# Seven block products for a pair of chunks in the first expert, half-wide products for the last group, and Silu in one instruction

## The chip, the cores and the metric

The kernel runs on one core of a Trainium2 chip. Its time is the device time of one execution in microseconds, and the median of three runs is compared. The profile is one more execution, taken by the hardware profiler.

## The reference, cut to what matters

Sliding-window attention with 8 heads gives 1536 tokens of width 512. They go through a first expert with 2048 hidden units, and its output goes through a second, gated expert with 1536 hidden units. All is float32.

```python
def _moe_ref(x, w_in, w_out):                       # x 1536x512, w_in 512x2048
    h = x @ w_in
    g = h * (1.0 / (1.0 + np.exp(-h)))              # silu
    return (g @ w_out).astype(np.float32)

def _moe2_ref(x, w_gate, w_val, w_out):             # w_gate, w_val 512x1536
    gate = 1.0 / (1.0 + np.exp(-(x @ w_gate)))
    val = x @ w_val
    return (gate * val @ w_out).astype(np.float32)
```

## The kernel before, in words

**Tiling.** The 1536 tokens are three groups of 512 columns (`NG` = 3, `G` = 512). Activations stand with the feature on the partition, in `X[g]`, four blocks of 128 features each (`KD` = 4). The hidden units are cut into chunks of 128: 16 in the first expert (`C1`), 12 in the second (`C2`). Every float32 operand is kept as a high and a low fp32r part, so one product of a 128x128 weight block with a 128x512 activation block is three matmuls (high by high, high by low, low by high). One chunk on one group is thus 4 x 3 = 12 matmuls up (`h_units`, L842) and 12 down.

**Stages.** Up to about 178 us the attention runs together with the first eight chunks of the first expert on groups 0 and 1 (`window`, L917). `phase_rest` (L960) does the rest: first the first eight chunks on group 2, then the last eight chunks group by group (`tasks`, L961 and 962), with `H` (up) two tasks ahead of `Y` (down). `Y` collects eight chunks in PSUM and evacuates once per group (`evac`, L1001). `act1` (L852) makes silu there as a Sigmoid on ScalarE and a multiply on VectorE.

**The second expert.** For each pair of chunks, `pair` (L1061) treats gate and val on groups 0 and 1 together as a 2x2 by 2x2 block product in seven instead of eight block products (Strassen's scheme in Winograd's form). The blocks are the two feature halves, the two chunks and the two groups. The sums of the weight blocks are made when the weights arrive (`split`, L451, into slots `SUMS`, L408), those of the activations in `evac`, into `T2`, `T3`, `T4` and `X[1]`, partly by GpSimd. A block product is six matmuls (`product`, L1043). `plain` (L1106) does gate and val on group 2 without that: 4 x 12 = 48 matmuls. `down` (L1116) is 24 matmuls for each group. The down product of group 2 is held back and mixed with the next `pair`.

**Weights.** `W` has 16 slots. A weight of 512 KB raw comes by SyncE into a stage buffer, is turned from float64 words into float32 and split in two (`to_f32`, `split`): two ScalarE and four VectorE instructions. The first 32 weights go round 16 slots, the others round 12 (`slots`, L400 to 402).

**Order.** The order on each engine is a list order that the program makes itself (`Issue.order`, L163): all instructions of a phase with their data dependences, each engine taking the one that can start first by the program's own cost figures. So TensorE doesn't follow the written order: where an operand isn't there, the next ready group of three matmuls goes ahead. All instructions are recorded on L260.

## Time and profile before

| | us |
|---|---|
| median of three runs (lowest to highest) | 646.38 (645.87 to 647.53) |
| the profiled execution | 646.85 |
| its span, first to last instruction | 645.1 |
| TensorE, VectorE, ScalarE, GpSimd busy | 634.1, 470.8, 307.5, 93.8 |

The span leaves out what lies around the program, 1.75 us in the profiled execution. Busy time counts overlapping instructions of an engine once; TensorE's is modelled at the ends of its matmuls, so the distance of their starts tells more than their length.

### The profile page before, as it was taken

What the parts mean: (1) busy time and instruction counts of PE and PEld (TensorE: products, weight loads), DVE (VectorE), ACT (ScalarE), POOL (GpSimd) and SP (SyncE); (2) the same over time, 40 slices, a digit from 0 to 9 for tenths busy, and PEclk for the clock granted to TensorE, in tenths of its full rate; (3) what the DMA queues carried; (4) which work ended last, traced back from release to release, by engine and by line L of the source; (5) the groups of instructions that cost most, each with busy time, mean ns of one, the idle gap of its engine ahead of it and who ended that gap; (6) DMA issues with size and microseconds to landing.
All of it is one profiled execution on the core that took longest, in us unless ns stands there. A gap on an engine that the chain in (4) does not pass through costs nothing.

```text
span 645.1 us, 9387 instructions
## 1 busy us (share of the span) xinstructions
PE 634.1 (98%) x3363; PEld 523.5 (81%) x3363; DVE 470.8 (73%) x1043; ACT 307.5 (48%) x648; POOL 93.8 (15%) x175
## 2 busy tenths in 40 slices
PE   9899999999999999999999999999999999999996
PEld 6689878787878888888888888888888888888884
DVE  6999996556268996252399897698889789864633
ACT  4898888655235653232255446553253343331210
POOL 5364545334110000000070000000000000000000
PEclk9899999999999999999999999999999999999999
DMA  8766562201014534000000303403123123100014
GB/s 215 193 156 191 171 178 51 51 19 35 0 34 126 167 108 142 13 1 2 0 1 5 126 28 104 132 24 107 65 66 93 39 66 98 34 0 1 0 45 156
DMA packets 65302, 49.05 MB, mean 76 GB/s; under 512 B 39648, under 2 KB 60128, under 8 KB 65248
## 3 DMA queue, kind: packets, MB, share of 16 engines
q1 hardware_dynamic: 64032, 48.11, 25.4%
q8 instruction: 28, 0.46, 0.3%
q10 hardware_dynamic: 1216, 0.26, 0.2%
q14 instruction: 26, 0.21, 0.1%
HBM read 45.22 MB, written 3.15 MB: 75 GB/s over the span
## 4 chain that ended last, share of the span: by engine, by line
PE 90%; DVE 6%; ACT 2%; issue 1%; POOL 1%; ACTq 0%; DVEq 0%
PE bank L260 89%; DVE u L260 2%; DVE t L260 1%; PE bank L1334 1%; DVE w L260 1%; POOL t L260 1%; ACT t L260 1%; DVE x L260 0%; DVE acc L260 0%; ACT kt L260 0%; DVE sg L260 0%; ACT u L260 0%; DVE ssum L260 0%; ACT pt L260 0%; DVE nm_all L260 0%
## 5 line engine op out<-in xcount | busy, mean ns | idle before, releaser
L260 PE MATMUL bank<-x,w 128*128 128x512 f32 (+1 forms) x1200 | 283.9, 383 | 0.0
L260 PEld LDWEIGHTS bank<-x,w 128*128 128x128 f32 x1200 | 218.4, 188 | 42.1 <-issue 0.5
L260 PE MATMUL bank<-g,w 128*128 128x512 f32 (+1 forms) x624 | 145.9, 377 | 0.4 <-DVE acc L260 0.4
L260 PEld LDWEIGHTS bank<-g,w 128*128 128x128 f32 x624 | 110.5, 188 | 22.6 <-DVE acc L260 0.8
L260 PE MATMUL bank<-w,g 128*128 128x512 f32 x432 | 105.5, 389 | 0.0
L260 PEld LDWEIGHTS bank<-w,g 128*128 128x128 f32 x432 | 80.9, 188 | 17.1 <-DVE acc L260 0.4
L260 DVE TENSOR_TENSOR acc<-acc,bank 128x512 f32<-128x512 f32 x96 | 65.2, 684 | 31.2 <-PE bank L260 30.3
L260 ACT ACTIVATE sg<-bank 128x512 f32<-128x512 f32 x66 | 39.3, 596 | 82.5 <-PE bank L260 81.3
L260 DVE SCALAR_TENSOR_TENSOR sg<-sg,bank 128x512 f32<-128x512 f32 x48 | 32.7, 682 | 53.8 <-ACT sg L260 53.8
L260 DVE SCALAR_TENSOR_TENSOR u<-stage,u 128x512 int32<-128x512 int32 x100 | 69.2, 696 | 0.9
L260 ACT ACTIVATE g<-sg 128x512 fp32r<-128x512 f32 x60 | 37.9, 632 | 43.3 <-DVE sg L260 24.8
L260 ACT ACTIVATE w<-u 128x512 fp32r<-128x512 f32 x62 | 38.8, 629 | 34.8 <-DVE u L260 22.4
L260 PE MATMUL bank<-t,w 128*128 128x512 f32 x216 | 54.0, 389 | 0.0
L260 POOL TENSOR_SCALAR t<-t,ssum 128x256 f32<-128x256 f32 (+1 forms) x88 | 46.6, 545 | 32.5 <-DVE ssum L260 30.4
L260 ACT ACTIVATE t<-t,nm_all 128x256 f32<-128x256 f32 (+1 forms) x96 | 45.9, 481 | 9.3 <-DVE nm_all L260 9.2
L260 DVE TENSOR_TENSOR w<-u,w 128x512 fp32r<-128x512 f32 x62 | 43.0, 695 | 6.6 <-ACT w L260 6.2
L260 PEld LDWEIGHTS bank<-t,w 128*128 128x128 f32 x216 | 40.6, 188 | 8.4
L260 DVE TENSOR_TENSOR m<-m,bank 128x512 f32<-128x512 f32 x48 | 32.4, 683 | 17.0 <-PE bank L260 16.6
L260 ACT ACTIVATE u<-stage 128x512 f32<-128x512 f32 x50 | 33.7, 673 | 20.6 <-DVE w L260 10.0
L260 DVE CUSTOM_DVE_ANT_0 t<-bank,mask 128x256 f32<-128x256 f32 (+1 forms) x96 | 34.6, 395 | 5.0 <-PE bank L260 3.5
L260 DVE TENSOR_TENSOR g<-sg,g 128x512 fp32r<-128x512 f32 x44 | 31.0, 705 | 9.2 <-ACT g L260 7.8
L260 ACT ACTIVATE w<-stage 128x512 fp32r<-128x512 f32 x30 | 18.7, 628 | 32.0 <-DVE stage L260 19.9
(94 smaller groups left out, 572.8 us busy)
## 6 DMA issues: line engine op xcount, KB each, us to landing
stage<-in_moe_w_out_dram SPq DMA_DIRECT2D x28, 512.0 KB, 3.7
stage<-in_moe_w_in_dram SPq DMA_DIRECT2D x16, 512.0 KB, 3.8
stage<-in_moe_w_gate_dram SPq DMA_DIRECT2D x12, 512.0 KB, 3.7
stage<-in_moe_w_val_dram SPq DMA_DIRECT2D x12, 512.0 KB, 3.7
v<-in_v_dram SPq DMA_DIRECT2D x12, 256.0 KB, 3.2
out_dram<-acc SPq DMA_DIRECT2D x12, 256.0 KB, 2.0
qk<-in_k_dram SPq DMA_DIRECT2D x11, 256.0 KB, 3.3
qk<-in_q_dram SPq DMA_DIRECT2D x11, 256.0 KB, 3.8
```

Source lines behind the costliest of these rows:

```text
L260: getattr(getattr(self.nc, o.eng), o.meth)(*o.args, **o.kw)
L1334: nc.tensor.matmul(bank[5][:, 0:256].rearrange("p (a b) -> p a b", a=2), warm, warm2, start=True, stop=True)
```

## The change

In the last eight chunks of the first expert, two chunks at a time, `first_pair` does groups 0 and 1 by seven block products, `first_single` does group 2 as before, and `first_down` does the down products of the three groups, adding to `accs` after each pair of chunks. The sums of the activations that this needs are made by `first_sums` during the stage before. For gate and val on group 2, `single` takes the place of `plain`: seven block products with the two halves of the group's columns, 256 each, as the column blocks; `last_sums` makes their activations. `seven` is the one scheme for all three; it keeps one PSUM bank for four of the seven products and copies it out by ScalarE between them. Its banks are turned from call to call. `act1` uses Silu in one instruction. The subtractions in `evac` go from GpSimd to VectorE. The weights after the first 16 go round nine slots. The diff, cut to its core:

```diff
--- before.py
+++ after.py
@@ -397,17 +404,21 @@
         for nm_, src, cut in (("gate", moe2_w_gate, colw), ("val", moe2_w_val, colw), ("o2", moe2_w_out, roww)):
             for j in range(2):
                 add_w((nm_, c + j), cut(src, c + j))
-    slots = [n % 16 for n in range(NW1)]
-    loop2 = [0, 1, 2, 3, 8, 9, 10, 11, 12, 13, 14, 15]
-    slots += [loop2[n % 12] for n in range(len(wsrc) - NW1)]
+    NRES = 2 * HA
+    slots = list(range(NRES))
+    loop = [0, 1, 2, 3, 8, 9, 10, 11, 12]
...
-    SUMS = {"gate": (4, 5), "val": (6, 7)}
-    sums_at = {nm_: max(held_by[sl] for sl in sl2) for nm_, sl2 in SUMS.items()}
-    sums_free = {"gate": -1, "val": -1}
+    LASTP = C1 // 2 - 1
+
+    def sums_in(nm_, p):
+        return {"in": (13, 14) if p == LASTP else (4, 5), "gate": (6, 7), "val": (4, 5)}[nm_]
+
+    sums_free = {"in": HA // 2 - 1, "gate": -1, "val": -1}
     wfree = [-1] * len(wsrc)
     wst = {"dma": 0, "split": 0, "on": False, "last": -100, "gap": 5, "wait": 8}
...
         if due is None:
             return True
         nm_, p = due
-        return wfree[sums_at[nm_]] >= 0 if p == 0 else sums_free[nm_] >= p - 1
+        if (nm_, p) == ("val", 0):
+            return sums_free["in"] >= LASTP - 1
+        if (nm_, p) in (("in", HA // 2), ("in", LASTP), ("gate", 0)):
+            return all(wfree[sl] >= 0 for sl in sums_in(nm_, p))
+        return sums_free[nm_] >= p - 1
 
     def to_f32(st, raw):
...
-            for f, sl in zip((b, a), SUMS[due[0]]):
+            for f, sl in zip((b, a), sums_in(*due)):
...
-        st = next(stage_r) if n < NW1 else st_all[n % 2]
+        st = next(stage_r) if n < NRES else st_all[(n + 1) % 2]
...
-            en.scalar.activation(out=sg, in_=ps, func=AF.Sigmoid)
-            en.vector.scalar_tensor_tensor(out=sg, in0=sg, scalar=2.0, in1=ps, op0=ALU.mult, op1=ALU.mult)
+            en.scalar.activation(out=sg, in_=ps, func=AF.Silu)
...
     def phase_rest(prev):
-        tasks = [(NG - 1, c) for c in halves1[0]]
-        tasks += [(g, c) for g in range(NG) for c in halves1[1]]
         accs = acc + [main2["acc2"]]
-        ybk = {}
-        yrot = [0]
-
-        def H(ti):
-            g, c = tasks[ti]
-            ps = bank[ti % 2]
-            for u in h_units(g, ("in", c), ps):
+        M = main2["M"]
+        yb = bank[2:6]
+
+        def H(c):
+            ps = bank[c % 2]
...
+        def Y(c):
...
+            gt = g_t.pop(c)
+            for d in range(KD):
+                mm3(yb[d], w, (slice(d * 128, (d + 1) * 128),), gt, (slice(0, G),), c == 0, c == HA - 1)
+                if c == HA - 1:
+                    en.scalar.activation(out=accs[2][:, d, :], in_=yb[d], func=AF.Copy, scale=2.0)
+                unit()
+            done_w(key)
...
+        def split2(dst, a):
+            en.scalar.activation(out=dst(0), in_=a, func=AF.Copy)
+            en.vector.tensor_tensor(dst(1), a, dst(0).bitcast(F32), ALU.subtract)
...
+        def first_sums(j):
+            a, b, c, d = M[0:4]
+            en.vector.tensor_tensor(a, *whole(X[0], j), ALU.add)
+            en.vector.tensor_tensor(b, *whole(X[1], j), ALU.add)
+            en.vector.tensor_tensor(a, b, a, ALU.subtract)
+            split2(lambda h: X[1][:, h, j, :], a)
+            en.vector.tensor_tensor(c, *whole(X[1], j + 2), ALU.add)
+            en.vector.tensor_tensor(b, c, b, ALU.subtract)
+            split2(lambda h: main2["T3"][:, h, j, :], b)
+            en.vector.tensor_tensor(c, c, a, ALU.subtract)
+            split2(lambda h: main2["T2"][:, h, j, :], c)
+            en.vector.tensor_tensor(d, *whole(X[0], j + 2), ALU.add)
+            en.vector.tensor_tensor(d, d, c, ALU.subtract)
+            split2(lambda h: main2["T4"][:, h, j, :], d)
...
+        def evac(last, g, d, ps):
+            a = accs[g][:, d, :]
+            en.vector.scalar_tensor_tensor(out=a, in0=ps, scalar=2.0, in1=a, op0=ALU.mult, op1=ALU.add)
+            if not last:
                 return
-            en.vector.tensor_tensor(a, a, ps, ALU.add)
-            if g != 1 or d > 1:
+            if g == 2:
+                cut = slice(0, 256) if d < 2 else slice(0, G)
+                halved(lambda h: X[g][:, h, d, cut], a[:, cut])
+                if d == 3:
+                    last_sums()
...
-                en.gpsimd.tensor_tensor(t, a, acc[0][:, d, :], ALU.subtract)
+                en.vector.tensor_tensor(t, a, acc[0][:, d, :], ALU.subtract)
                 halved(lambda h: X[1][:, h, d, :], t)
             else:
-                en.gpsimd.tensor_tensor(t, a, t, ALU.subtract)
+                en.vector.tensor_tensor(t, a, t, ALU.subtract)
                 halved(lambda h: main2["T2"][:, h, j, :], t)
...
+        def last_sums():
+            a = main2["acc2"]
+            le, ri = a[:, :, 0:256], a[:, :, 256:512]
+            t, t3 = [M[i].rearrange("p (a b) -> p a b", a=2) for i in (6, 3)]
+            en.vector.tensor_tensor(t, ri[:, 0:2], le[:, 0:2], ALU.subtract)
+            halved(lambda h: X[2][:, h, 0:2, 256:512], t)
+            en.vector.tensor_tensor(t, ri[:, 2:4], t, ALU.subtract)
+            halved(lambda h: main2["H2"][:, h], t)
+            en.vector.tensor_tensor(t3, ri[:, 2:4], ri[:, 0:2], ALU.subtract)
+            halved(lambda h: main2["H3"][:, h], t3)
+            en.vector.tensor_tensor(t, le[:, 2:4], t, ALU.subtract)
+            halved(lambda h: main2["H4"][:, h], t)
...
-        make_flag(bank[5])
+        make_flag(bank[6])
...
-        n, done = len(tasks), 0
-        for ti in range(1, n):
-            H(ti)
-            while done <= ti - 2:
-                for _ in Y(done):
-                    pass
-                done += 1
-        late = [y for ti in range(done, n) for y in (Y(ti),)]
-        second_expert((u for y in late for u in y), accs)
-
-    def second_expert(pending, accs):
+        for c in range(1, HA):
+            H(c)
+            if c in (2, 4):
+                first_sums(c // 2 - 1)
+            if c > 1:
+                Y(c - 2)
+        Y(HA - 2)
+        Y(HA - 1)
+        pair_loops(accs, evac)
+
+    def pair_loops(accs, evac):
...
+        def seven(names, p, b, bs, t1, t2, t3, done):
+            w = [[wtile((nm_, 2 * p + j)) for j in range(2)] for nm_ in names]
+            s = [[W[sl] for sl in sums_in(nm_, p)] for nm_ in names]
+            end = len(names) - 1
+            n = b["11"].shape[-1]
+            m1, m2, m3 = [[x[:, 0:n] for x in y] for y in bs]
+
+            def p1(i):
+                yield from product(m1[i], w[i][0], 0, b["11"], True)
+                copy(t1[i], m1[i])
+
+            def p6(i):
+                yield from product(m1[i], s[i][1], 0, b["t2"], False)
+                copy(t2[i], m1[i])
+
+            def p5(i):
+                yield from product(m2[i], s[i][0], 256, b["t1"], True)
+
+            def p7(i):
+                yield from product(m1[i], s[i][0], 0, b["t3"], False)
+                copy(t3[i], m1[i])
+                add(t3[i], t3[i], m2[i])
+                if i == end:
+                    done("22")
+
+            def p2(i):
+                yield from product(m3[i], w[i][0], 256, b["21"], True)
+                add(t1[i], t1[i], m3[i])
+                if i == end:
+                    done("11")
+
+            def p4(i):
+                yield from product(m1[i], w[i][1], 256, b["t4"], False)
+                if i == end:
+                    done("21")
+
+            def p3(i):
+                yield from product(m2[i], s[i][1], 256, b["22"], False)
+                add(t2[i], t2[i], m2[i])
+                if i == end:
+                    done("12")
+
+            if end:
+                order = (p1, 0), (p1, 1), (p6, 0), (p6, 1), (p5, 0), (p7, 0), (p5, 1), (p7, 1), (p2, 0), (p2, 1)
+                order += (p4, 0), (p4, 1), (p3, 0), (p3, 1)
+            else:
+                order = (p1, 0), (p5, 0), (p6, 0), (p2, 0), (p7, 0), (p4, 0), (p3, 0)
+            for f, i in order:
+                yield from f(i)
+
...
+        blocks = {
+            "11": X[0][:, :, 0:2, :], "21": X[0][:, :, 2:4, :], "t1": X[1][:, :, 0:2, :], "22": X[1][:, :, 2:4, :],
+            "t2": T2, "t3": T3, "t4": T4,
+        }
+        last = X[2]
+        halves = {
+            "11": last[:, :, 0:2, 0:256], "21": last[:, :, 2:4, 0:256], "t1": last[:, :, 0:2, 256:512],
+            "22": last[:, :, 2:4, 256:512], "t2": main2["H2"], "t3": main2["H3"], "t4": main2["H4"],
+        }
+        def first_pair(p, gts):
+            need_w(("in", 2 * p + 1))
+            bs = banks()[0:3]
+            bs = [(x[0],) for x in bs]
+            t = {"11": M[4], "12": M[0], "22": M[2], "21": M[6]}
+
+            def done(k):
+                sg, gt = t[k], gts[int(k[1]) - 1, int(k[0]) - 1]
+                en.scalar.activation(out=sg, in_=bs[0][0] if k == "21" else sg, func=AF.Silu)
+                split_g(gt, sg)
+
+            yield from seven(("in",), p, blocks, bs, [t["11"]], [t["12"]], [t["22"]], done)
+            sums_free["in"] = p
+
+        def first_single(p):
+            for j, ps in enumerate((bank[3], bank[4])):
+                for u in h_units(NG - 1, ("in", 2 * p + j), ps):
+                    u()
+                    yield unit()
+                en.scalar.activation(out=M[1 + 2 * j], in_=ps, func=AF.Silu)
+
+        def first_down(p, g, gts):
+            keys = [("out", 2 * p + j) for j in range(2)]
+            for d in range(KD):
+                yb = bank[6 + d % 2] if p == C1 // 2 - 1 and g == NG - 1 else bank[5 + ny[0] % 3]
+                ny[0] += 1
+                for j, key in enumerate(keys):
+                    need_w(key)
+                    mm3(yb, wtile(key), (slice(d * 128, (d + 1) * 128),), gts[g, j], (slice(0, G),), j == 0, j == 1)
+                    if d == KD - 1 and j == 1 and g == NG - 1:
+                        done_w(keys[0])
+                        done_w(keys[1])
+                    yield unit()
+                evac(p == C1 // 2 - 1, g, d, yb)
...
-            c = 2 * p
             for nm_ in ("gate", "val"):
-            for i in range(2):
-                yield from product(bs[i][0], w[i][0], 0, X[0], 0, True)
-                en.scalar.activation(out=tc_[i], in_=bs[i][0], func=AF.Copy)
-            for i in range(2):
-                yield from product(bs[i][1], s[i][1], 0, T2, 0, True)
-                add(tu[i], tc_[i], bs[i][1])
-            for i in range(2):
-                yield from product(bs[i][2], s[i][0], 256, X[1], 0, True)
-            for i in range(2):
-                yield from product(bs[i][1], s[i][0], 0, T3, 0, False)
-                add(tv[i], tc_[i], bs[i][1])
-                add(tv[i], tv[i], bs[i][2])
-                if i == 0:
...
-        def plain(p, gts):
-            for j, (b, m) in enumerate(((1, 3), (2, 5))):
-                for nm_, ps in (("gate", bank[b]), ("val", bank[3 + b])):
-                    for u in h_units(NG - 1, (nm_, 2 * p + j), ps):
-                        u()
-                        yield unit()
-                    if nm_ == "gate":
-                        en.scalar.activation(out=M[m], in_=ps, func=AF.Sigmoid)
-                en.vector.tensor_tensor(M[m], M[m], ps, ALU.mult)
+                need_w((nm_, 2 * p + 1))
+            bs = banks()
+            t = {"11": M[4:6], "12": M[0:2], "22": M[2:4], "21": (M[6], bs[0][1])}
+
+            def done(k):
+                sg, val = t[k]
+                sig(sg, bs[0][0] if k == "21" else sg)
+                glu(gts[int(k[1]) - 1, int(k[0]) - 1], sg, val)
+
+            yield from seven(("gate", "val"), p, blocks, bs, t["11"], t["12"], t["22"], done)
+        def single(p):
+            bs = banks()
+            le, ri = slice(0, 256), slice(256, 512)
+            g0, v0, g1, v1 = M[2], M[3], M[6], M[4]
+
...
+            yield from seven(
+                ("gate", "val"), p, halves, bs, (g0[:, le], v0[:, le]), (g0[:, ri], v0[:, ri]), (g1[:, ri], v1[:, ri]), done
+            )
+            for nm_ in ("gate", "val"):
+                sums_free[nm_] = p
+                for j in range(2):
+                    done_w((nm_, 2 * p + j))
+
+        turn = [0]
+
+        def banks():
+            k = [(i - turn[0]) % 3 for i in range(3)]
+            turn[0] += 1
+            return [(bank[x], bank[3 + x]) for x in k]
...
+        gts = {(1, 1): gr[0], (1, 0): gr[1], (0, 1): gr[2], (0, 0): gr[3], (2, 0): gr[2], (2, 1): gr[3]}
+        pending = iter(())
+        for p in range(HA // 2, C1 // 2):
+            for _ in first_pair(p, gts):
+                next(pending, None)
+            every(pending)
+            tail = p == C1 // 2 - 1
+            if not tail:
+                every(first_single(p))
+            every(first_down(p, 0, gts))
+            if not tail:
+                split_g(gts[2, 0], M[1])
+                split_g(gts[2, 1], M[3])
+            every(first_down(p, 1, gts))
+            if tail:
+                every(first_single(p))
+                split_g(gts[2, 0], M[1])
+                split_g(gts[2, 1], M[3])
+            pending = first_down(p, 2, gts)
         for p in range(C2 // 2):
-            gts = {(1, 1): gr[0], (1, 0): gr[1], (0, 1): gr[2], (0, 0): gr[3], (2, 0): gr[2], (2, 1): gr[3]}
             for _ in pair(p, gts):
                 next(pending, None)
-            for _ in pending:
-                pass
-            for _ in plain(p, gts):
-                pass
-            for g in range(NG - 1):
-                for _ in down(p, g, gts):
-                    pass
-                if g == 0:
-                    split_g(gts[2, 0], M[3])
-                    split_g(gts[2, 1], M[5])
+            every(pending)
+            every(single(p))
+            every(down(p, 0, gts))
+            split_g(gts[2, 0], M[2])
+            split_g(gts[2, 1], M[6])
+            every(down(p, 1, gts))
             pending = down(p, NG - 1, gts)
-        for _ in pending:
-            pass
+        every(pending)
...
+        for i, nm_ in enumerate(("H2", "H3", "H4")):
+            main2[nm_] = W[13 + i].rearrange("p h (a b) -> p h a b", a=2)
```

## Rows read from the trace of the kernel before

**Rows 1.** The page, parts 1 and 2: engine shares; granted TensorE clock by slice.

```profile
PE 634.1 (98%) x3363; PEld 523.5 (81%) x3363; DVE 470.8 (73%) x1043; ACT 307.5 (48%) x648; POOL 93.8 (15%) x175
...
PEclk9899999999999999999999999999999999999999
```

**Rows 2.** The chain of waits from 160 us: start, length, engine, tile.

```profile
159.77 479.41 PE bank L260 x2136
...
639.21 0.69 DVE acc L260
```

**Rows 3.** Waits from 361 to 640 us: total, times, longest.

```profile
PEld bank L260 <- DVE acc L260: 0.4, 2, 0.2
```

**Rows 4.** Timeline of TensorE in the second expert: start, length, instruction, count.

```profile
375.05 16.48 PE L260 MATMUL bank<-x,w 128*128 128x512 f32 x72
391.37 5.60 PE L260 MATMUL bank<-w,g 128*128 128x512 f32 x24
```

**Rows 5.** Busy time by stretch: each engine, PEclk, DMA share, GB/s.

```profile
195.53:239.05 43.52, 43.52 (x193) 36.05 (x192) 41.26 (x71) 25.09 (x41) 0.00 (x0) 1.00 0.43 133
451.21:497.45 46.24, 46.24 (x205) 38.30 (x204) 40.58 (x73) 18.77 (x33) 0.00 (x0) 1.00 0.21 69
```

**Rows 6.** Timeline of TensorE where 256-column matmuls run, 60 to 66 us.

```profile
59.84 0.88 PE L260 MATMUL bank<-x,w 128*128 128x256 f32 x6
60.56 0.60 PE L260 MATMUL bank<-ident,t 128*128 128x128 f32 x4
...
63.94 1.67 PE L260 MATMUL bank<-x,w 128*128 128x256 f32 x12
...
65.53 0.70 PE L260 MATMUL bank<-kt 64*128 64x256 f32 x4
```

**Rows 7.** Groups by form, whole span: busy, mean ns of one, idle before.

```profile
L260 PEld LDWEIGHTS bank<-x,w 128*128 128x128 f32 x1200 | 218.4, 188 | 42.1 <-issue 0.5
...
L260 ACT ACTIVATE m<-bank 128x512 f32<-128x512 f32 x12 | 7.2, 599 | 20.6 <-PE bank L260 20.6
...
L260 ACT ACTIVATE kt<-bank 128x256 f32<-128x256 f32 x24 | 9.1, 381 | 6.9 <-PE bank L260 4.9 <-DVE kt L260 1.9
...
L260 DVE SCALAR_TENSOR_TENSOR sg<-sg,bank 128x512 f32<-128x512 f32 x48 | 32.7, 682 | 53.8 <-ACT sg L260 53.8
...
L260 DVE TENSOR_TENSOR acc<-acc,bank 128x512 f32<-128x512 f32 x96 | 65.2, 684 | 31.2 <-PE bank L260 30.3
...
L260 POOL TENSOR_TENSOR m<-acc,m 128x512 f32<-128x512 f32 x4 | 6.7, 1673 | 2.5 <-DVE t L260 1.9 <-ACT t L260 0.7
```

**Rows 8.** Timeline of ScalarE at its second table load.

```profile
178.05 1.28 ACT L260 ACT_TABLE_LOAD   x1
...
179.48 0.60 ACT L260 ACTIVATE sg<-bank 128x512 f32<-128x512 f32 x1 [0.15 <-POOL g L260]
```

**Rows 9.** Timeline of VectorE, two short stretches.

```profile
343.31 0.41 DVE L260 TENSOR_TENSOR u<-u 128x256 f32<-128x256 f32 x1
343.64 0.68 DVE L260 TENSOR_TENSOR w<-u,w 128x512 fp32r<-128x512 f32 x1
...
628.64 0.68 DVE L260 TENSOR_TENSOR acc<-acc,bank 128x512 f32<-128x512 f32 x1
629.24 0.69 DVE L260 TENSOR_TENSOR g<-m,g 128x512 fp32r<-128x512 f32 x1
```

**Rows 10.** Timeline of SyncE: first and last of six issues of first-expert weights.

```profile
182.68 10.08 SPq L260 DMA_DIRECT2D stage<-in_moe_w_in_dram  x2
...
225.54 3.21 SPq L260 DMA_DIRECT2D stage<-in_moe_w_out_dram  x2
```

**Rows 11.** Timeline of TensorE's weight loads in the stretch of rows 6.

```profile
63.91 1.49 PEld L260 LDWEIGHTS bank<-x,w 128*128 128x128 f32 x12
```

More of the change, by code (lines that the diff above doesn't have):

```diff
@@ L112 @@
         "rc": 0.195, "cr": 0.147}
+FUNCS = {AF.Exp: "exp", AF.Silu: "silu", AF.Sigmoid: "sigmoid"}
 class Issue:
@@ L232, in order @@
                 else:
+                    f = FUNCS.get(o.kw.get("func"), self.funcs) if e == "scalar" else self.funcs
+                    if f != self.funcs:
+                        self.funcs, o.start = f, o.start + 1.28
                     free[e] = o.start + o.occ
@@ L423, in sums_due @@
     def sums_due(n):
+        if n < NRES:
+            return None
+        if n < NW1:
+            p, j = divmod(n, 4)
+            return ("in", p) if j == 1 else None
         p, j = divmod(n - NW1, 6)
-        return (("gate", p) if j == 1 else ("val", p)) if n >= NW1 and j in (1, 3) else None
+        return (("gate", p) if j == 1 else ("val", p)) if j in (1, 3) else None
     def can_split(n):
@@ L452, in split @@
         w = W[slots[n]]
-        st = next(u_r) if n < NW1 else u_all[n % 4]
+        st = next(u_r) if n < NRES else u_all[n % 4]
         to_f32(st, stages.pop(n))
@@ L491, in pump_w @@
         n = wst["dma"]
-        if n < len(wsrc) and n - wst["split"] < (3 if n < NW1 else 2) and slot_free(n):
+        if n < len(wsrc) and n - wst["split"] < (3 if n < NRES else 2) and slot_free(n):
             dma_w(n)
@@ L1051, in product, with copy, add, sig @@
                 yield unit()
+        def copy(o, a):
+            en.scalar.activation(out=o, in_=a, func=AF.Copy)
+        def add(o, a, b):
+            en.vector.tensor_tensor(o, a, b, ALU.add)
+        def sig(o, a):
+            en.scalar.activation(out=o, in_=a, func=AF.Sigmoid)
+        def mul(o, a, b):
+            en.vector.tensor_tensor(o, a, b, ALU.mult)
+        def seven(names, p, b, bs, t1, t2, t3, done):
[39 more added lines that the diff above has]
+                yield from f(i)
         def glu(gt, sg, val):
@@ L1061, in pair @@
         def pair(p, gts):
-            c = 2 * p
             for nm_ in ("gate", "val"):
-                need_w((nm_, c + 1))
-            w = [[wtile((nm_, c + j)) for j in range(2)] for nm_ in ("gate", "val")]
-            s = [[W[sl] for sl in SUMS[nm_]] for nm_ in ("gate", "val")]
-            bs = [bank[0:3], bank[3:6]]
-            tu, tv, tc_ = M[0:2], M[2:4], M[4:6]
-            add = lambda o, a, b: en.vector.tensor_tensor(o, a, b, ALU.add)
-            sig = lambda o, a: en.scalar.activation(out=o, in_=a, func=AF.Sigmoid)
@@ L1086, in pair @@
-            glu(gts[1, 1], tv[0], tv[1])
-            for i in range(2):
-                yield from product(bs[i][1], w[i][1], 256, T4, 0, False)
-                add(tc_[i], tc_[i], bs[i][1])
-                if i == 0:
-                    sig(tc_[0], tc_[0])
-            glu(gts[0, 1], tc_[0], tc_[1])
-            for i in range(2):
-                yield from product(bs[i][2], s[i][1], 256, X[1], 2, False)
-                add(tu[i], tu[i], bs[i][2])
-                sums_free[("gate", "val")[i]] = p
-                if i == 0:
-                    sig(tu[0], tu[0])
```

61 lines of the change are left out of this document (27 added, 34 removed).

## The prediction

> **What bounds the kernel now.** I read the engine shares first, then the chain of waits, then the timeline of TensorE, and the other engines only where the change loads them. TensorE is busy 98% of the span at the full granted clock (2.4 GHz) in all but one early slice [rows 1]. The chain that ends last is one piece of matmuls from 159.8 to 639.2 us and then one evacuation [rows 2]. The reader should see that in those 479 us no other engine ends a wait that matters: all that held TensorE after 361 us is two waits of 0.2 us each on an evacuation [rows 3]. So after 160 us time is the number of matmuls times their distance, and whatever other engines gain or lose there counts only if it makes TensorE wait. The distance comes from starts, since the lengths overlap: 72 matmuls of 512 columns lie between 375.05 and 391.37 us, so 16.32 / 72 = 226.7 ns each [rows 4]. VectorE is the engine with least room, 40.6 of 46.2 us in one round of the second expert and 41.3 of 43.5 us in the stage where weights come fastest [rows 5]. Even at that second share TensorE didn't wait.
>
> **Seven products in the first expert.** For two chunks on two groups there are 8 x 6 = 48 matmuls up now, and 7 x 6 = 42 then. Group 2 and the down products keep theirs. Four pairs of chunks make 4 x 6 = 24 fewer, 24 x 226.7 ns = 5.44 us, all on the path that sets the end.
>
> **Seven products of halves.** `plain` has 48 matmuls of 512 columns in each of six rounds, 48 x 0.2267 = 10.88 us. `single` has 14 products of 6, so 84 matmuls, of 256 columns. Half the work isn't half the time: six 256-column matmuls of the same fp32r form start from 59.84 and the next thing starts at 60.56, 0.72 / 6 = 120 ns each, not 113 [rows 6]. 84 x 0.120 = 10.08 us, a gain of 0.80 a round and 4.80 us in six. The bounds: exactly half of 226.7 is 113.3 ns, 9.52 us, gain 8.2 in all; twelve that carry a restart after transposes and a turn to another form take 65.53 - 63.94 = 1.59 us, 132.5 ns each, 11.13 us, a loss of 1.5 in all [rows 6]. I take 120, since a run of 84 has a turn only at its ends. Break-even is 10.88 / 84 = 129.5 ns, so this half of the change hangs on 10 ns.
>
> The Trainium skill (TensorE: Matmul & The Clock Gate, Back-to-back issue gap) gives N/2.4 + 2.5 ns for a warm matmul alone, 215.8 and 109.2 ns here; by it the two gains would be 5.2 and 7.1 us, 12.3 together. The trace disagrees on both, 226.7 and 120, and I go by the trace.
>
> **Sum of TensorE.** 5.44 + 4.80 = 10.24 us.
>
> **Silu.** Each of the 32 sigmoid activations of the rest of the first expert loses the multiply behind it, 0.68 us on VectorE [rows 7]; Silu I price as the Sigmoid. It may need a table of its own: one load more, 1.28 us on ScalarE, after which the next instruction starts 0.15 later [rows 8]. ScalarE is busy 18.8 of 46.2 us [rows 5]. Value nothing, bounds 0 and 1.4 us; what hides it is that the first products of the second expert wait on no Sigmoid. Without that cover it is 1.4 us once.
>
> **VectorE in a round of the second expert.** Instructions of 512 start 0.60 apart, of 256 0.33 apart [rows 9]. Gone are four of ten additions and two products of `plain`; new are one product of 512, six additions and two products of 256. That is -5 x 0.60 + 8 x 0.33 = -0.4, so 40.2 of 45.4 us. Not a bound. ScalarE gains four copies of 0.60 and six nearest to the 0.38 of a 256-column copy [rows 7], +4.7 us, to about 23.5 of 45.4.
>
> **VectorE in the stage that makes the first sums.** `first_sums` is 24 instructions, 14.4 us. Against it go 8 multiplies of Silu (4.8), and weights: twelve are fetched in that stage now, two for each issue [rows 10], four are needed by then. A weight costs VectorE 3 x 0.60 + 0.33 = 2.1 us, so eight later ones free 17, and one set of sums of weights costs 4 x 0.33 + 2 x 0.60 = 2.5. 41.3 + 14.4 - 4.8 - 17 + 2.5 = 36.4 of 43.5 us: nothing. If the weights come as early as now, it is 53 us and up to 10 us of stall, but nothing forces them ahead.
>
> **VectorE in the four pairs.** 138 matmuls are 31.3 us. Three additions, six low parts and twelve evacuations are 21 x 0.60 = 12.6 us; four weights and a set of sums are 11.1. 23.7 of 31.3. `first_down` evacuates after every pair of chunks and turns over three banks, so each evacuation of 0.68 us has the two other banks' products, 2 x 1.36 us, to hide it. Nothing.
>
> **New waits.** In `seven` the bank of product 1 is copied before product 6 may add to it, again before 7 and before 4. A copy is 0.60 us [rows 7]. The other product between is 1.36 us wide (0.72 in `single`, copy 0.38), and where there is none (7 and 4 of `first_pair`) ready group-2 products go ahead in the list order. Behind a waiting copy on ScalarE stand the splits of weights, which are needed pairs later. Sums of weights for the next round can be written only when `single` has read the last ones (now: when `pair` has): four steps, 2.4 us on VectorE, with 48 down matmuls (10.9 us) that hide them together with their own eight evacuations and two low parts, 6.0. So the value of all this is a small leftover. Nearest is what such a reuse leaves now, 0.2 us in a few places [rows 3]; I take a quarter of it, 0.05, for each of ten `seven` stretches, 0.5 us. Bounds: nothing, and 0.6 for each, 6 us.
>
> **Nine slots, GpSimd to VectorE.** Next-round gate and the first val still have slots a round ahead; only the second val and the down weights wait for `single`, and a down weight has 30 us. The fetches that move stand alone in SyncE's queue, and the DMA engines are busy 43% and 21% in those stretches [rows 5]. GpSimd's subtractions (1.67 us) become 0.6 on VectorE [rows 7, 9]; they count in the handover below. All else (attention, `window`, the last down and its write) is untouched.
>
> **The number.** Profiled execution: span 645.1 - 10.24 + 0.5 = 635.4, with the 1.75 around it 637.1. The median of before lies 0.47 under the profiled time, so the median after is 646.38 - 9.74 = 636.6.
>
> **Rivals.** (1) Handover. Groups 0 and 1 now finish 5.4 us before `pair` begins; before, a whole group of eight chunks lay between. After its last down product group 1 has 22 VectorE instructions, 13.2 us, begun 4.1 us earlier, so 9.1 us after it alone. `first_single` must put its Silu into buffers that this chain reads, so group 2's down and its banks wait too. TensorE has 5.44 + 2 x 1.36 + 1.36 = 9.5 us that need none of it. If two weights and a set of sums (6.8 us) fall in between, TensorE waits 6.4: 643.0, still faster. For it: VectorE is full there. Against: the stage at 95% without a wait [rows 5], and the list puts the chain first.
>
> (2) The gain is eaten. Waits of 0.6 us in all ten `seven` stretches and half of (1): 636.1 + 6 + 3.2 = 645.3, no change. Against: ready work nearly everywhere.
>
> (3) Slower, copies. In `single` a product lasts only 0.72 us, and the copy takes 0.38 plus the way there and back. If ScalarE is behind a 0.6 us split each time and the list has nothing ready, each of six handings-on in a round waits 0.4: 6 x 6 x 0.4 = 14.4 us, 636.1 + 14.4 = 650.5. It decides from 0.28 us each on, 10.24 / 36. Against: ScalarE is half idle, and down products of groups 0 and 1 are ready.
>
> (4) Slower, weight loads. A 256-column matmul gives a load 120 ns, and a load is recorded at 188 ns [rows 7]. If that were its real distance, `single` takes 84 x 0.188 = 15.8 us, 4.9 more than `plain`: 636.6 + 4.8 + 29.5 = 670.9. It decides from 129.5 ns. Against: twelve loads in 1.49 us, 124 ns each, with the matmuls [rows 11]. The Trainium skill (TensorE: Matmul & The Clock Gate, LDWEIGHTS) puts a load at columns/1.2, 107 ns for 128; by that the load fits with 13 ns to spare.
>
> (5) The change doesn't do what it says: turns inside `single` keep the halves at 132.5 ns and nothing is won there: 646.38 - 5.44 + 1.5 + 0.5 = 642.9.
>
> **How the numbers follow.** Forecast 0.70; (1) 0.12, (5) 0.05, (2) 0.06, (3) 0.04, (4) 0.03. A measurement of this kernel can tell about 0.3%, 1.9 us, from no change. Faster by more: 0.70 + 0.12 + 0.05 = 0.87; within: 0.06; slower: 0.07. Low end: halves at 113.3 ns and no leftover, 646.38 - 5.44 - 8.2 = 632.7, taken as 633. High end: (1) and (5), 643. Outside lie (2) to (4), 0.13.
>
> **What would show it.** Right: 256-column runs in six places, 84 x 120 ns each; 226.7 ns elsewhere; the chain still matmuls to the end; TensorE's busy time about 10 us less; no GpSimd after 190 us; VectorE near 88% in the rounds. Wrong: gaps before the first `pair` (1), waits of TensorE on ScalarE copies (3), starts over 130 ns in the halves (4, 5).

## The result, and the profile after

The changed kernel takes 636.36 us (median of four runs, 635.73 to 637.68), the kernel before, run beside it, 646.61; the ratio is 0.9844, with a 95% interval of 0.9827 to 0.9861, so it is 1.6% faster. 636.6 was forecast. The profiled execution is one of 637.68 with a span of 635.9; 637.1 and 635.4 were forecast for it.

The page of the changed kernel, parts 1 and 2, against [rows 1] (all its instructions are recorded on L267):

```profile
PE 624.0 (98%) x3555; PEld 525.0 (83%) x3555; DVE 501.7 (79%) x1137; ACT 354.9 (56%) x751; POOL 80.0 (13%) x167
...
PEclk9999999999999999999999999999999999999999
```

TensorE's busy time fell by 10.1 us, GpSimd's ends with the attention, and the clock is full in every slice. VectorE and ScalarE have more work in less time. The two timelines, of the changed kernel's TensorE in a first-expert pair and in one round's `single`, against [rows 4] and [rows 6]:

```profile
276.99 11.04 PE L267 MATMUL bank<-g,w 128*128 128x512 f32 x48
287.87 0.84 PE L267 MATMUL bank<-x,w 128*128 128x512 f32 x3
...
422.19 1.68 PE L267 MATMUL bank<-w,w 128*128 128x256 f32 x12
...
426.58 1.60 PE L267 MATMUL bank<-x,w 128*128 128x256 f32 x12
428.02 1.60 PE L267 MATMUL bank<-w,w 128*128 128x256 f32 x12
429.46 1.60 PE L267 MATMUL bank<-x,w 128*128 128x256 f32 x12
430.90 0.86 PE L267 MATMUL bank<-w,g 128*128 128x512 f32 x3
```

From 276.99 to 287.87 there are 48 matmuls, 226.7 ns each as before. From 426.58 to 428.02 there are 12 of 256 columns, 120 ns each as forecast; the whole `single` reaches from 420.75 (12 matmuls before the 422.19 of the third line) to 430.90, 10.15 us for 84, with one wait of 0.08 in it. The chain that ends last still ends in matmuls and one evacuation, now at 629.85 [rows 2]. Here are the attention's last products in the timelines of the kernel before and of the changed one, and the last piece of the changed kernel's chain:

```profile
160.84 1.97 PE L260 MATMUL bank<-pt,v 128*64 128x128 f32 x32
```

```profile
160.60 1.97 PE L267 MATMUL bank<-pt,v 128*64 128x128 f32 x32
```

```profile
629.85 0.69 DVE acc L267
```

From those products to the last evacuation it is 639.21 - 160.84 = 478.37 us before and 629.85 - 160.60 = 469.25 after: 9.12 less. I call this stretch TensorE's chain below. It leaves out the start of the program, which ends between 159.2 and 161.5 us in the profiles of this study, and what follows the last evacuation.

What TensorE's weight loads (PEld) waited for after 185 us, against [rows 3]:

```profile
PEld bank L267 <- ACT m L267: 0.6, 2, 0.4
PEld bank L267 <- DVE acc L267: 0.5, 2, 0.3
PEld bank L267 <- issue: 0.3, 2, 0.2
```

In this stretch the kernel before has, beside the two of [rows 3], one wait of 0.3 us on GpSimd.

And busy time by stretch, against [rows 5]: first sums, two of the four pairs, the handover (the end of the first expert and the start of the second), and two rounds of the second expert. A line gives the busy time of PE, PEld, DVE, ACT and POOL, then the granted clock, the DMA share and GB/s.

```profile
195.13:238.75 43.62, 43.62 (x193) 35.88 (x191) 32.58 (x60) 23.29 (x40) 0.00 (x0) 1.00 0.28 85
240.25:271.55 31.30, 31.30 (x140) 25.93 (x138) 24.91 (x43) 15.00 (x26) 0.00 (x0) 1.00 0.22 68
302.83:335.47 32.64, 32.64 (x146) 27.05 (x144) 27.72 (x49) 16.41 (x28) 0.00 (x0) 1.00 0.29 92
335.47:376.69 41.22, 41.22 (x187) 34.01 (x186) 40.72 (x71) 28.72 (x51) 0.00 (x0) 1.00 0.08 26
422.19:467.72 45.53, 45.53 (x243) 39.42 (x241) 40.48 (x76) 23.37 (x42) 0.00 (x0) 1.00 0.27 82
558.80:604.35 45.55, 45.55 (x243) 39.36 (x241) 30.94 (x55) 18.64 (x34) 0.00 (x0) 1.00 0.00 1
```

The waits are few but more than before. In the handover, from 335.47 to 376.69, VectorE is busy 40.72 of 41.22 us.

### The profile page after: what moved, and what is told of

Its sections match the earlier page's. It is cut to its first block, busy times and chain, and to the rows that moved or that the text cites. A ratio compares the mean times of both kernels' runs of the same rounds, so it can differ in the third digit from the quotient of the medians.

```text
span 635.9 us, 9940 instructions
## 1 busy us (share of the span) xinstructions
PE 624.0 (98%) x3555; PEld 525.0 (83%) x3555; DVE 501.7 (79%) x1137; ACT 354.9 (56%) x751; POOL 80.0 (13%) x167
## 4 chain that ended last, share of the span: by engine, by line
PE 91%; DVE 5%; ACT 2%; issue 1%; POOL 1%; ACTq 0%; DVEq 0%
PE bank L267 90%; DVE t L267 1%; DVE u L267 1%; ACT t L267 1%; PE bank L1499 1%; POOL t L267 1%; DVE w L267 1%; ACT kt L267 0%; ACT u L267 0%; DVE x L267 0%; DVE kt L267 0%; DVE acc L267 0%; ACT pt L267 0%; DVE sg L267 0%; DVE mask L267 0%
## 5 line engine op out<-in xcount | busy, mean ns | idle before, releaser
L267 PE MATMUL bank<-x,w 128*128 128x512 f32 (+1 forms) x1104 | 238.0, 355 | 0.0
L267 PEld LDWEIGHTS bank<-x,w 128*128 128x128 f32 x1104 | 183.6, 189 | 27.8 <-issue 0.5
L267 PE MATMUL bank<-g,w 128*128 128x512 f32 (+1 forms) x624 | 145.5, 377 | 0.0
L267 PEld LDWEIGHTS bank<-g,w 128*128 128x128 f32 x624 | 110.7, 188 | 21.7 <-issue 0.7
L267 PE MATMUL bank<-w,g 128*128 128x512 f32 x432 | 105.7, 390 | 0.0
L267 PEld LDWEIGHTS bank<-w,g 128*128 128x128 f32 x432 | 80.5, 188 | 16.8 <-issue 0.3
L267 DVE TENSOR_TENSOR acc<-acc,bank 128x512 f32<-128x512 f32 x84 | 57.4, 684 | 32.7 <-PE bank L267 32.3
L267 ACT ACTIVATE m<-bank 128x512 f32<-128x512 f32 (+1 forms) x80 | 40.9, 516 | 68.8 <-PE bank L267 66.9
L267 PE MATMUL bank<-t,w 128*128 128x512 f32 x288 | 74.8, 390 | 0.0
L267 PEld LDWEIGHTS bank<-t,w 128*128 128x128 f32 x288 | 53.9, 188 | 11.5 <-ACT m L267 0.4
L267 DVE SCALAR_TENSOR_TENSOR u<-stage,u 128x512 int32<-128x512 int32 x84 | 58.4, 697 | 0.5
L267 DVE TENSOR_TENSOR m<-m,bank 128x512 f32<-128x512 f32 (+1 forms) x72 | 40.7, 572 | 18.4 <-ACT m L267 11.1
L267 ACT ACTIVATE w<-u 128x512 fp32r<-128x512 f32 x62 | 38.9, 627 | 26.9 <-DVE u L267 23.7
L267 ACT ACTIVATE t<-t,nm_all 128x256 f32<-128x256 f32 (+1 forms) x96 | 45.9, 482 | 10.8 <-DVE nm_all L267 10.7
L267 ACT ACTIVATE sg<-bank 128x512 f32<-128x512 f32 (+1 forms) x52 | 28.5, 548 | 39.5 <-PE bank L267 38.9
L267 POOL TENSOR_SCALAR t<-t,ssum 128x256 f32<-128x256 f32 (+1 forms) x88 | 44.8, 524 | 34.3 <-DVE ssum L267 22.4
L267 DVE TENSOR_TENSOR w<-u,w 128x512 fp32r<-128x512 f32 x62 | 43.1, 695 | 3.0 <-ACT w L267 2.7
L267 DVE SCALAR_TENSOR_TENSOR acc<-bank,acc 128x512 f32<-128x512 f32 x48 | 32.5, 686 | 10.1 <-PE bank L267 9.7
L267 DVE CUSTOM_DVE_ANT_0 t<-bank,mask 128x256 f32<-128x256 f32 (+1 forms) x96 | 34.4, 394 | 4.7 <-PE bank L267 3.3
L267 ACT ACTIVATE g<-sg 128x512 fp32r<-128x512 f32 x40 | 25.2, 631 | 21.8 <-DVE sg L267 12.3
L267 DVE SCALAR_TENSOR_TENSOR stage<-stage,stage 128x512 int32<-128x512 int32 x52 | 35.5, 683 | 0.2
L267 DVE TENSOR_TENSOR g<-m,g 128x512 fp32r<-128x512 f32 x44 | 29.9, 686 | 7.0 <-ACT g L267 6.6
```

Of the source, the lines that this page charges most:

```text
L267: getattr(getattr(self.nc, o.eng), o.meth)(*o.args, **o.kw)
```

## The experiments

All are edits of the changed kernel; each diff shows its core. Ratios are to the kernel before, in brackets the 95% interval; that of the changed kernel is 0.9844. The times are medians of runs that spread over up to 3 us, while the chain is read from one profiled execution of each kernel. The changed kernel's profiled execution, 637.68 us, is the slowest of its four, so differences of medians to it come out 0.5 to 2.6 us above those of the profiled executions. For a small cost the chain is the better measure.

**plain_last** puts the 48 products of 512 columns back for the last group (the call of `last_sums` is left out).

```diff
         def single(p):
             bs = banks()
...
-            yield from seven(
-                ("gate", "val"), p, halves, bs, (g0[:, le], v0[:, le]), (g0[:, ri], v0[:, ri]), (g1[:, ri], v1[:, ri]), done
-            )
+            for j, m in enumerate((M[2], M[6])):
+                for nm_, ps in zip(("gate", "val"), bs[j]):
+                    for u in h_units(NG - 1, (nm_, 2 * p + j), ps):
+                        u()
+                        yield unit()
+                    if nm_ == "gate":
+                        sig(m, ps)
+                mul(m, m, ps)
```

> Gate and val on the last group go back to 48 products of 512 columns a round; the rest is the changed kernel. My theory (time is the number of matmuls times their distance, and 84 x 120 ns replaced 48 x 226.7 ns): 6 x 0.80 = 4.8 us come back, 636.4 + 4.8 = 641.2, 640.7 to 641.8. Rival, halves win nothing and the 10 us are from somewhere else (Silu, freed VectorE time): 636.4, within 0.7. Rival, halves cost half (113 ns): 644.5.

641.31 us, ratio 0.9933 [0.9917, 0.995]; chain 473.32, so 4.07 longer, from the attention's last products to the last evacuation:

```profile
159.17 1.97 PE L267 MATMUL bank<-pt,v 128*64 128x128 f32 x32
```

```profile
632.49 0.69 DVE acc L267
```

My theory holds. By count the chain should grow by 288 x 226.7 - 504 x 120 ns = 4.81 us. It grew by 0.74 less, and that is waits that went with the halves. In the changed kernel the starts of matmuls after 186 us stand more than 70 ns too far apart at twelve places: five of 0.08 us in `single`, two of 0.1 in its last round, and five of 0.1 at the first pair and in the handover, 1.12 us in all. In plain_last there are four, at the first pair and in the handover, and in the kernel before none.

**eight_first** undoes the first expert's products, **neither** does that and the edit of plain_last.

```diff
         def first_pair(p, gts):
-            yield from seven(("in",), p, blocks, bs, [t["11"]], [t["12"]], [t["22"]], done)
+            for i, (g, j) in enumerate(((0, 0), (0, 1), (1, 0), (1, 1))):
+                ps, sg = bs[i % 3][0], M[(4, 0, 2, 6)[i]]
+                for u in h_units(g, ("in", 2 * p + j), ps): ...
+                en.scalar.activation(out=sg, in_=ps, func=AF.Silu)
+                split_g(gts[g, j], sg)
...
-            if c in (2, 4):
-                first_sums(c // 2 - 1)
```

> The four pairs of the first expert take eight block products again, and the sums of the activations for them are not made; the weight sums still are. My theory: 24 x 226.7 ns = 5.4 us come back, 641.8, 641.3 to 642.5. Rival, the gain is from Silu and the lighter VectorE: 636.4 or less, since the activation sums (24 VectorE instructions) are gone as well.

> Both sets of seven products are undone; what stays of the change is Silu, evacuation after each pair of chunks, nine slots, no GpSimd and the new order. My theory: all of these are worth nothing, 636.4 + 10.2 = 646.6, within 1.0 of the kernel before. Rival, they carry part of the gain: below 645.

eight_first: 644.96 us, ratio 0.9973 [0.9962, 0.9985]; neither: 647.40, 1.0013 [1.0003, 1.0022]. The two ends of eight_first's chain:

```profile
160.16 1.97 PE L267 MATMUL bank<-pt,v 128*64 128x128 f32 x32
```

```profile
634.69 0.69 DVE acc L267
```

In both, half of group 2's hidden units are those of the next pair, which changes values and the order of a few instructions: group 2 shares `gr[2]` and `gr[3]` with group 0, which is written first here, while group 2's down products are still pending. The chains are 474.53 and 478.44. So eight products cost 5.28 more on the chain (5.44 by count, less 0.16 of waits that went), and with both undone it has the 478.37 of the kernel before to 0.1 us: in this order of instructions Silu, evacuation per pair, nine slots and the rest move it by nothing in sum. As whole times the two are 8.6 and 11.0 us above the changed kernel, 3 and 1 more than forecast, so both forecasts of the time missed, neither's barely. The profiled executions are only 5.96 and 10.34 apart from the changed kernel's. Of eight_first's 5.96, 5.28 are the chain, 1.1 lie behind the last evacuation (7.2 us to the end of the span instead of 6.1), and the start of the program is 0.4 shorter. The other 2.6 us of its median are spread between executions: the changed kernel's profiled one is its slowest, eight_first's is one of its fastest.

**eight_first2** and **neither2** write group 1 first, as the changed kernel does; the diff is against eight_first and neither.

```diff
-            for i, (g, j) in enumerate(((0, 0), (0, 1), (1, 0), (1, 1))):
-                ps, sg = bs[i % 3][0], M[(4, 0, 2, 6)[i]]
+            for i, (g, j) in enumerate(((1, 1), (1, 0), (0, 1), (0, 0))):
+                ps, sg = bs[i % 3][0], M[(2, 0, 6, 4)[i]]
```

> As eight_first, but the four products of a pair of chunks go in the order of the buffers that they fill (group 1 first), so the down product of group 2, which is mixed in, has read its hidden units before they are written over; in eight_first it read half of them too late and got the next pair's. My theory: 24 x 226.7 ns come back, less the few tenths of a us that the changed kernel waits at these products: 641.3 to 642.2. Rival, eight_first's 645 was the price of eight products and not of the wrong order: 644.5 and up.

> As neither, in the same mended order. My theory: Silu, evacuation after each pair, nine slots and no GpSimd together are worth nothing: 646.0 to 647.0 against 646.4 to 647.1 of the kernel before. Rival, they carry part of the gain: below 645.

648.89 us, ratio 1.0042 [1.0027, 1.0057], and 651.88, 1.0086 [1.0065, 1.0107]. Both expectations missed, and the reason is the main find here. In the handover of eight_first2, the timelines of ScalarE and of TensorE:

```profile
364.81 1.28 ACT L267 ACT_TABLE_LOAD   x1
366.10 0.63 ACT L267 ACTIVATE m<-m 128x512 f32<-128x512 f32 x1
366.75 1.28 ACT L267 ACT_TABLE_LOAD   x1
368.04 1.09 ACT L267 ACTIVATE m<-bank 128x512 f32<-128x512 f32 x2
```

```profile
364.81 1.54 PE L267 MATMUL bank<-x,w 128*128 128x512 f32 x6
368.69 2.51 PE L267 MATMUL bank<-x,w 128*128 128x512 f32 x6 [2.34 <-ACT m L267]
371.00 1.48 PE L267 MATMUL bank<-t,w 128*128 128x512 f32 x3
372.29 1.02 PE L267 MATMUL bank<-g,w 128*128 128x512 f32 x3
```

The group of the table loads over the whole program, and the stretches:

```profile
L267 ACT ACT_TABLE_LOAD x5 | 6.4, 1283 | 2.8 <-issue 2.7
```

```profile
368.69:372.68 3.99, 3.99 (x11) 3.12 (x12) 2.51 (x5) 3.92 (x6) 0.00 (x0) 0.57 0.40 133
372.68:376.00 3.32, 3.32 (x16) 2.75 (x15) 1.97 (x4) 0.42 (x1) 0.00 (x0) 1.00 0.00 0
```

The list put a Sigmoid of the second expert between Silus of the first. Each change between the two is a table load of 1.28 us here, so the two Silus that free the banks of `first_single` stand behind 364.81 to 368.04, and TensorE starts again at 368.69 after 2.3 us of nothing. Then it runs at a granted clock of 0.57 of full for 4 us; from 371.00 to 372.29 it is 0.50, which is 1.2 instead of 2.4 GHz. Of the chain's 9.72 us over the changed kernel, 2.5 are the wait (starts at 365.96 and 368.69, less one distance), 1.5 the half clock (11 matmuls in 3.99 us, of 0.2267 each at full), and 5.7 remain for the products, 5.44 by count. neither2 has the same place and the same five loads, a wait as long with the clock at half behind it, and a chain of 482.91, 4.54 over the kernel before. So the rest of the change is worth nothing only where the order keeps the two functions apart. The changed kernel, eight_first and neither have three loads.

**sigmoid** makes silu of Sigmoid and a VectorE product again, at three places; one of them:

```diff
-            en.scalar.activation(out=sg, in_=ps, func=AF.Silu)
+            en.scalar.activation(out=sg, in_=ps, func=AF.Sigmoid)
+            en.vector.tensor_tensor(sg, sg, ps, ALU.mult)
```

> Silu is made again by Sigmoid on ScalarE and a product on VectorE, 32 more VectorE instructions of 0.60 us; the products stay as changed, and the table load goes. My theory: nothing but the handover feels it, where VectorE is already 99% busy in the profile; six of the 32 fall there, up to 3.6 us of wait: 636.4 to 640. Rival, Silu matters everywhere: 32 x 0.68 = 22 us more, 655 and up.

638.82 us, ratio 0.9887 [0.9871, 0.9904]; chain 471.08, 1.83 longer, with two table loads. The timeline in the handover (VectorE, ScalarE, TensorE) and the busy time up to it:

```profile
372.68 0.69 DVE L267 TENSOR_TENSOR sg<-acc,sg 128x512 f32<-128x512 f32 x1
373.28 0.69 DVE L267 SCALAR_TENSOR_TENSOR w<-m,w 128x512 fp32r<-128x512 f32 x1
373.40 0.63 ACT L267 ACTIVATE w<-sg 128x512 fp32r<-128x512 f32 x1 [0.57 <-DVE sg L267]
...
374.06 0.60 ACT L267 ACTIVATE m<-bank 128x512 f32<-128x512 f32 x1
...
374.71 0.74 PE L267 MATMUL bank<-t,w 128*128 128x512 f32 x2 [1.61 <-ACT m L267]
```

```profile
335.50:372.80 37.30, 37.23 (x169) 30.70 (x169) 37.19 (x66) 23.23 (x40) 0.00 (x0) 1.00 0.10 29
```

One wait of 1.6 us at 374.71 carries the difference. A product of the first `pair` waits for a copy of its bank on ScalarE (374.06). By the code that copy goes into `M[3]`, which `last_sums` uses as well, and VectorE reads it until 373.97. ScalarE's own instruction before the copy ends at 374.03, and it had waited for VectorE's of 372.68. The two ends are 0.06 us apart, so which of them held the copy isn't told; both go back to VectorE. It is busy 37.19 of the 37.30 us up to there, so it comes to this late.

**tail_early** takes the special order of the last pair away.

```diff
-            tail = p == C1 // 2 - 1
+            tail = False
```

> In the last pair of the first expert the up products of the last group go ahead of the down products again, as in the other pairs, so nothing stands between the end of groups 0 and 1 and the second expert but the down products of group 2. My theory (the handover is on the edge, VectorE 99% busy, and those 5.4 us of products are its cover): a wait of 1 to 5 us in front of or in the first pair, 637.5 to 641.5. Rival, the list order finds enough to do anyway: 636.4 within 0.7.

638.58 us, ratio 0.9866 [0.9849, 0.9882]; chain 469.98, 0.73 longer. The median lies in the range of the theory, but the wait itself is smaller than the 1 to 5 us named: one of 0.7, ended by VectorE, at the first half-wide product. The chain that ends last goes back from it on VectorE alone, from 373.43 to before 360. TensorE's timeline:

```profile
371.25 1.55 PE L267 MATMUL bank<-x,w 128*128 128x512 f32 x6
373.48 0.97 PE L267 MATMUL bank<-x,w 128*128 128x256 f32 x6 [0.68 <-DVE m L267]
```

**pool_sums** gives the subtractions of the activation sums back to GpSimd, four such lines; one of them:

```diff
-                en.vector.tensor_tensor(t, a, acc[0][:, d, :], ALU.subtract)
+                en.gpsimd.tensor_tensor(t, a, acc[0][:, d, :], ALU.subtract)
```

> The eight subtractions of the activation sums for the second expert go back to GpSimd, 1.3 to 1.7 us each in the kernel before against 0.60 on VectorE. They stand in the handover. My theory (a chain of group 1's last two blocks sets it, three subtractions each): 3 x 1 us longer for each, of which TensorE's other work covers most: 636.4 to 639. Rival, the handover is short of VectorE time and not of the chain: 4.8 us less VectorE make it 635.5 to 636.

642.64 us, ratio 0.9941 [0.9924, 0.9958]; chain 474.12, 4.87 longer (4.90 between the profiled executions). Both expectations missed. TensorE waits 2.7 us, and again five table loads stand in the profile, two of them in front of the Silus that end that wait; afterwards the clock is at 0.64. The timelines of ScalarE and TensorE, and the busy time of the stretch after the wait:

```profile
359.08 1.28 ACT L267 ACT_TABLE_LOAD   x1
360.38 0.63 ACT L267 ACTIVATE m<-m 128x512 f32<-128x512 f32 x1
360.91 0.62 ACT L267 ACTIVATE t<-m 128x512 fp32r<-128x512 f32 x1
361.55 1.28 ACT L267 ACT_TABLE_LOAD   x1
362.84 1.09 ACT L267 ACTIVATE m<-bank 128x512 f32<-128x512 f32 x2
```

```profile
363.49 4.61 PE L267 MATMUL bank<-x,w 128*128 128x512 f32 x12 [2.71 <-ACT m L267]
```

```profile
363.49:368.17 4.68, 4.68 (x14) 3.69 (x15) 3.13 (x6) 4.65 (x8) 0.00 (x0) 0.64 0.46 132
```

ScalarE has no gap from 358.46, where it copies a bank, to the Silu that ends the wait at 363.44, and the two loads are 2.57 of these 5.0 us. But the Silus write `M[1]` and `M[3]`, which by the code the last subtractions use too, and VectorE reads the last result of GpSimd from 361.57 to 362.25. So a longer chain on GpSimd and the changes of table come together here, and what each would have cost alone stays open.

**dve4**, **dve12** and **dve24** add VectorE work in five rounds of the second expert.

```diff
                     en.vector.tensor_tensor(a, a, yb, ALU.add)
+                if p < C2 // 2 - 1 and g in (0,):        # dve12, dve24: (0, 1, 2)
+                    en.vector.tensor_tensor(a, a, a, ALU.max)   # dve24: twice
```

> Four more VectorE instructions of 0.60 us in each of the first five rounds of the second expert, each behind an evacuation (the result is the same). VectorE is busy 40.4 of 45.5 us there, so 42.8. My theory, VectorE has 5 us of room a round and TensorE sets the time: 636.4, at most 0.7 more. Rival, VectorE already holds part of the round: 5 x 2.4 = 12 us more.

> Twelve instead of four, 7.2 us a round: 47.6 us of VectorE against 45.5 of TensorE. My theory: the bound changes sides, about 2 us in each of four rounds and 0 in the last, plus what the order loses, 642 to 648. Rival, VectorE busy time overstates its load and there is more room: 637.

> Two more VectorE instructions of 0.60 us behind every evacuation in five rounds, 24 a round, 72 us in all (the result is the same). The five rounds of the changed kernel hold 190 us of VectorE in 228 us. My theory, that is all the room there is, and weights' work drifts to where VectorE is idle: 190 + 72 = 262, 34 us over, so 636.4 + 34 = 670, 664 to 676. Rival, VectorE overlaps with itself and busy time overstates it: under 650.

638.18 us, ratio 0.9856 [0.9839, 0.9872]; 637.41, 0.9854 [0.9833, 0.9875]; 664.13, 1.0278 [1.0257, 1.03]. The chains are 469.29, 469.79 and 496.03. So 12 and 36 us of VectorE cost TensorE 0.04 and 0.54, and 72 us cost 26.8. My 642 to 648 for dve12 was wrong: it took every round by itself, but the list moves VectorE's work into the last round, which had room. Busy time by round, the last two of dve12 and one of dve24:

```profile
513.26:559.01 45.75, 45.75 (x242) 39.33 (x241) 45.36 (x86) 22.95 (x42) 0.00 (x0) 1.00 0.23 70
559.01:604.65 45.64, 45.64 (x242) 39.28 (x241) 44.11 (x82) 20.22 (x37) 0.00 (x0) 1.00 0.12 35
```

```profile
517.00:570.00 53.00, 48.09 (x238) 39.37 (x237) 51.83 (x96) 22.09 (x41) 0.00 (x0) 0.97 0.18 59
```

The changed kernel's VectorE is busy 30.94 us in its last of these rounds (558.80 to 604.35), dve12's 44.11. Five rounds have 228 us and held 190; 36 more fit, 72 don't, by 34. 27 of the 34 were paid; where the other 7 found room stays open. By the median dve4 misses its forecast, 638.18 where at most 637.1 was allowed; its chain and its profiled execution, 0.04 and 0.5 us longer, fit.

**quarter** computes only half of the last group's columns in `single`.

```diff
-            "11": last[:, :, 0:2, 0:256], "21": last[:, :, 2:4, 0:256], "t1": last[:, :, 0:2, 256:512],
+            "11": last[:, :, 0:2, 0:128], "21": last[:, :, 2:4, 0:128], "t1": last[:, :, 0:2, 256:384],
...
-            le, ri = slice(0, 256), slice(256, 512)
+            le, ri = slice(0, 128), slice(256, 384)
```

> The 84 products of the last group on half of their columns, 128 instead of 256; the other half is left out, so the result of the last group is not the reference's. It shows what sets the distance at 256. If a matmul costs its columns and a fixed part, (N + 32)/2.4 ns as 226.7 and 120 give: 66.7 ns, 84 x 53 ns = 4.5 us a round, 27 in all, 609.5, unless VectorE holds it (40 of 41 us then), so 609 to 614. If the weight load sets a floor near what 128-column transposes keep (109 ns): 5.5 us in all, 631. If the floor is already at work at 256: 636.

632.40 us, ratio 0.9768 [0.9751, 0.9784]; chain 464.84, 4.41 shorter. TensorE's timeline in one round's `single`:

```profile
425.61 1.50 PE L267 MATMUL bank<-x,w 128*128 128x128 f32 x12
426.95 1.50 PE L267 MATMUL bank<-w,w 128*128 128x128 f32 x12
428.29 1.50 PE L267 MATMUL bank<-x,w 128*128 128x128 f32 x12
```

Twelve of 128 columns take 1.34 us, 111.7 ns, where the line through 226.7 and 120 would give 66.7. I read that as a floor; with one width below 256 that isn't shown. If the floor is the same at 256, it lies some 8 ns under the 120.

## Why the prediction was right, point by point

**The count and the distance** held to a hundredth: 226.7 and 120 ns, 24 matmuls and six rounds. By count that is 10.25 us, and plain_last and eight_first give 4.07 and 5.28 on the chain for each by itself, where 4.81 and 5.44 are the counts. The 109 ns that the Trainium skill (TensorE: Matmul & The Clock Gate, Back-to-back issue gap) gives for a warm matmul of 256 columns alone isn't seen. Rival (4) is off, but not by far: quarter's 128 columns keep 111 ns. The 107 ns that the Trainium skill has for a load of 128 columns (the same page, LDWEIGHTS) is near that distance.

**The time** agrees better than its parts. The chain is 9.12 us shorter and the profiled execution 9.17, where 9.74 was forecast; the medians are 10.25 apart. That 636.36 lies 0.2 from 636.6 is in part luck: the forecast put the median after 0.47 under its profiled execution, as before, and it lies 1.32 under it.

**The leftover** was mis-sized: 0.5 us forecast, 1.13 measured, the 10.25 by count less the 9.12 by which the chain got shorter. The waits are the twelve named at plain_last: five at the first copied bank of `single`, two in its last round, and five at the first pair of the first expert and in the handover. The table of waits puts the weight loads' longest, 0.4 and 0.3 us, on ScalarE's copies and on evacuations.

**VectorE and ScalarE.** A round has 40.5 us of VectorE in 45.5 (40.2 in 45.4 forecast) and 23.4 of ScalarE (23.5). The first sums took 32.6 us of 43.6 where 36.4 was worked out, and two errors hide in that: nine of the 22 recorded instructions of `first_sums` run before 195 us, where VectorE is busy without a gap, and seven weights are prepared in the stretch, not four. The pairs took 24.9 to 27.7 of 31 to 32.6, where 23.7 was worked out; the second of them prepares six weights and not four. None ends a wait that matters; dve12 shows that the five rounds together hold 36 us more.

**Silu, valued at nothing**, was wrong in kind. In this kernel it is worth 1.8 us on the chain (471.08 - 469.25) and 2.5 by medians. The products that it saves VectorE cost no wait in the pairs, but those near the handover do. And the table load was bounded at 1.4 us, once: that holds only as long as the list keeps the last Silu ahead of the first Sigmoid, which nothing in the change demands. Where it didn't, ScalarE loaded twice within 4 us.

**GpSimd to VectorE** was put into the handover without a price; it is worth 4.9 us on the chain of this kernel (6.3 by medians, 642.64 - 636.36). How much of that is GpSimd's and how much the order with two more table loads, which came with it, stays open.

**Rival (1), the handover**, named the right place. VectorE is 99% busy there, and tail_early, sigmoid, pool_sums and eight_first2 each made TensorE wait, by 0.7 to 2.7 us. In the first two VectorE is behind the wait, as the rival has it; in the last two the wait ends with a Silu behind two table loads, which no rival names. In the changed kernel no start of a matmul there is later by more than 0.1 us. That fits the reason given, enough products that need none of it: with fewer of them ready, in tail_early, the wait of 0.7 appears. (2), (3) and (5) were not seen; of (3) there is one wait of 0.08 us in a round, not six of 0.4.

## What to carry to other kernels

Where one engine holds the whole chain, count its instructions and take their distance from the starts of the same form; that gave the gain of two rearrangements to within the new waits, 10.25 by count and 9.12 on the chain. Judge an engine beside it over the whole stretch in which its work may move: VectorE at 95 to 99% in five rounds cost 0.5 us here (dve12), and at 99% in one handover it cost 1.8 us as soon as work was added there (sigmoid). Before a second ScalarE function comes near another, see what keeps the two apart in the order, since every alternation between Silu and Sigmoid was a table load ahead of whatever else ScalarE had to free.

## What the runs showed of the hardware

A wait of TensorE cost more than itself: after 2.3 us of nothing in eight_first2 and 2.7 in pool_sums the granted clock was 0.57 and 0.64 over the next 4.0 and 4.7 us. Within that, matmuls of 512 columns stood 430 ns apart (three between 371.00 and 372.29, granted clock 0.50), so 1.2 instead of 2.4 GHz. After the waits of 0.7 and 1.6 us in tail_early and sigmoid the distance stayed 227 and the clock full. A table load took 1.28 us, and in eight_first2 the next instruction started 0.01 us behind it. fp32r matmuls stand 226.7, 120 and 111 ns apart for 512, 256 and 128 columns. Silu costs ScalarE what Sigmoid does: from PSUM 599 ns in the changed kernel and 595 in sigmoid, both from 186 to 235 us.
